# Head outputs of a unit gathered in one tile and turned by four DMA transposes in a two-layer transformer kernel

## The chip, the cores and the metric

The kernel runs on one core of a Trainium2 chip. The metric is the time of one execution on the device, in microseconds. The profile is of one such execution.

## What is computed

Two transformer layers that share their weights, on 2048 tokens of 512 features, all in bf16. Each layer is an attention block (32 heads of 16 features) and a feed-forward block (1376 hidden features), each with a residual. Both blocks normalize their input, the feed-forward block twice.

```python
def _A_ref(x, wqkv, wo):
    B, S, D = x.shape
    H = 32; Dh = D // H
    qkv = (x @ wqkv).reshape(B, S, 3, H, Dh).transpose(2, 0, 3, 1, 4)
    q, k, v = qkv[0], qkv[1], qkv[2]
    scores = jnp.einsum("bhqd,bhkd->bhqk", q, k) * Dh ** -0.5
    p = _softmax(scores, axis=-1)
    o = jnp.einsum("bhqk,bhkd->bhqd", p, v)
    return o.transpose(0, 2, 1, 3).reshape(B, S, D) @ wo

def _B_ref(x, w1, b1, w2, b2):
    h = _gelu(_layernorm(x) @ w1 + b1)
    return h @ w2 + b2

for layer in range(2):
    x = x + _A_ref(_layernorm(x), A_wqkv, A_wo)
    x = x + _B_ref(_layernorm(x), B_w1, B_b1, B_w2, B_b2)
```

## The kernel before

**Who sets the order.** No instruction's place is written by hand. The jobs of the kernel are Python generators that hand tasks to a list scheduler (`Sched`, L271) while the kernel is built. The scheduler keeps a model of each engine with the durations that every task is given, always takes the task that can begin first and, among those ready, the one of lowest priority number (`best`, L380), and so lays out five fixed instruction streams (PE, ACT, DVE, POOL, and SP, the queue of the DMAs). On the chip each stream runs in its order, with semaphore waits where tiles are passed on. A DMA counts in the model as done after its issue time, its latency and a margin of 1.0 us (L25, L126). When the plan is complete, it is run through again, and zero matmuls (`zw`, L1260) are put into the gaps of PE[...].

**Units and segments.** The two attention blocks are called L=1 and L=3. A unit is a set of query tiles of 128 tokens: four units of four tiles in L=1, three of four and two of two in L=3, so 9 in all. A segment is one unit and one head group `hg` of four heads; each unit has eight. In the first unit of each layer the keys come in two parts.

**Scores and exponentials.** For a segment, PE computes scores with keys on the partitions, 128 keys by 512 queries at a time, four heads beside each other in rows of 32 (L1354). ACT takes the exponential of two or three such score tiles per instruction (L1339). Keys of the blocks 3, 6, 9, 12 and 15 can also go to DVE, which forms an approximate exponential out of the bits: one load of the score tile (L1431, `d_load`), then three shifted copies (L1462, `job_d`). Whether it does is decided by `take_d` (L1364) as the plan is laid: it needs DVE to be free within 1.3 us and little work waiting on it, and a free PSUM bank. A tile that DVE doesn't take is left to ACT.

**Values.** PE multiplies the exponentials with the values and a column of ones, 17 output rows per head, in four columns of 32 (L1528). So bank 6 of PSUM holds, for head `hp` of the group, 16 features and the sum of the weights on partitions 32·hp to 32·hp+16, for up to 512 queries. A tile of ACT takes one such product, a tile of DVE four.

**End of a segment** (`job_segend`, L1551). DVE turns the bank in 32x32 blocks into `accT` (L1558): queries on the partitions, features along the row. In the units whose keys come in two parts, POOL keeps the first part's sums in `OT` (L1577) and adds them (L1586 to L1589). Then DVE takes the reciprocal of the weights' sum (L1591), multiplies (L1596) into one of two buffers `ob` whose rows have 16 features and 16 zeros per head, and turns that in 32x32 blocks back into `OT[:, hg, :]` (L1598). The key `oproj` of the unit before holds these steps back until that unit's projection has been planned.

**Output projection** (`job_post`, L1609). When the eight head groups of a unit are turned, PE contracts for each 128 tokens eight planes of `OT` with eight planes of `wo` (L1622). Both have 128 rows, of which 64 are zeros. DVE adds the residual (L1624). The norm, the turn of the normed rows by a DMA (L1647), and the feed-forward block (L1655, L1679, L1685, L1693) follow, beside the next unit's scores. The unit's result then feeds the QKV projection of the second layer (L900), whose keys are stored and loaded turned (`job_kload`, L1136), or the output.

**The last unit** (`job_tail`, L1710). Its feed-forward block can't hide behind scores. It begins when the unit before is done and head groups 0 to 6 are turned; `tail_tile` (L1749) brings the residual into PSUM by an identity matmul (L1754) and adds the eight products of the projection (L1758), of which the last waits for head group 7.

Of the kernel before, what the change touches and what calls it, by code (L numbers as in the profile page):

```python
# [8 lines left out]
BF16 = mybir.dt.bfloat16  # L9
F16 = mybir.dt.float16  # L10
F32 = mybir.dt.float32
# [3 lines left out]
ALU = mybir.AluOpType  # L15
# [244 lines left out]
def I(fn, reads=(), writes=(), dur=0.3, same_ok=(), lat=None):  # L260
    return (fn, tuple(reads), tuple(writes), tuple(same_ok), dur, lat)
# [236 lines left out]
class Builder:  # L498
# [44 lines left out]
    def alloc(self, es):  # L543
# [5 lines left out]
        self.wo = t("wo", [128, 8, 512], BF16)  # L549
# [28 lines left out]
        self.ob = t("ob", [128, 2, 512], BF16)  # L578
# [31 lines left out]
        pl = self.S_.pools  # L610
# [13 lines left out]
        pl["ob"] = Pool([])  # L624
# [105 lines left out]
    def build_startup_late(self):  # L730
# [4 lines left out]
        def fills():  # L735
# [8 lines left out]
            yield f(lambda e: e.memset(self.ob[:, :, :], 0.0), [("ob", 0), ("ob", 1)], 1.3)  # L744
            for k in range(2):
                S_.release("ob", k)
# [4 lines left out]
            yield f(lambda e: e.memset(self.wo[:, 0:4, :].rearrange("p a b -> p (a b)").bitcast(F32), 0.0), [("wo0",)], 1.0)  # L751
            yield f(lambda e: e.memset(self.wo[:, 4:8, :].rearrange("p a b -> p (a b)").bitcast(F32), 0.0), [("wo0",)], 1.0)
# [4 lines left out]
            wor = self.A_wo.rearrange("(g h d) n -> h d g n", h=4, d=16)  # L757
            for hp in range(4):
                yield ld(lambda e, hp=hp: e.dma_start(self.wo[32 * hp:32 * hp + 16, :, :], wor[hp]), [("wo0",)], [("wo", hp)])
            S_.mark(("wld",))  # L760
# [790 lines left out]
    def job_segend(self, sg):  # L1551
# [40 lines left out]
        if self.prev(L, qc):  # L1592
            yield ("keys", [("oproj",) + self.prev(L, qc)])
        o = yield ("get", "ob")
        ob = self.ob[:, o, 0:W].rearrange("p (b r) -> p b r", r=32)
        yield Task("dve", 1.2, [I(lambda e: e.tensor_tensor(out=ob[:, :, 0:16], in0=T[:, :, 0:16], in1=rv.unsqueeze(2).broadcast_to([128, nb, 16]), op=ALU.mult), [RA, ("rv", a)], [("ob", o)], 0.147 + 0.268 * W / 512)])  # L1596
        S_.release("accT", a)
        yield Task("dve", 1.2, [I(lambda e: e.transpose(self.OT[:, hg, 0:W], self.ob[:, o, 0:W]), [("ob", o)], [("OT", hg)], 0.17 + 0.53 * W / 512)])  # L1598
        S_.release("ob", o)
# [3 lines left out]


# [4 lines left out]
    def job_post(self, L, qc):  # L1609
        S_ = self.S_  # L1610
        pr = self.post_prio(L, qc)
        tiles = self.units[L][qc]
        W = 128 * len(tiles)
        if L == 3 and qc == len(self.units[L]) - 1:
            yield from self.job_tail(L, qc)
            return
        yield ("keys", [("ot", L, qc, hg) for hg in range(8)])
        for i, tt in enumerate(tiles):
            yield ("ready", "pe", [("OT", hg) for hg in range(8)])
# [90 lines left out]
    def job_tail(self, L, qc):  # L1710
# [8 lines left out]
        yield ("keys", [("post",) + self.prev(L, qc)] + [("ot", L, qc, hg) for hg in range(7)])  # L1719
        slot = yield ("get", "lnc")  # L1720
# [28 lines left out]
    def tail_tile(self, L, qc, tt, slot, i, left):  # L1749
# [5 lines left out]
        for h0 in range(8):  # L1755
            if h0 == 7:
                yield ("keys", [("ot", L, qc, 7)])
            yield Task("pe", pr if h0 == 7 else 1.5, [I(lambda e, hg=h0: e.matmul(self.ps[:, b, :], lhsT=self.OT[:, hg, i * 128:(i + 1) * 128], rhs=self.wo[:, hg, :], start=False, stop=(hg == 7), skip_group_check=True),  # L1758
                                                        [("OT", h0)] + [("wo", k) for k in range(4)], [("ps", b)], 0.216, [("ps", b)])])
# [112 lines left out]
```

## Time and profile before

| | before |
|---|---|
| Median of 3 runs | 1634.3 us (1631.6 to 1636.0) |
| Span of the profiled execution | 1629.9 us |
| Exponentials on ACT (L1339) | 1302 instructions |
| Score tiles taken by DVE (L1431) | 874 |
| Turns from `ob` to `OT` on DVE (L1598) | 72 |
| Matmuls with `wo` (L1622 and L1758) | 256, of 379 ns from issue to end |
| DMA transposes `xnT`, `yT` (128x512) | 70, 2.5 us from issue to landing |

A line of a group names the source line, the engine, the operation, what it writes and reads with the shapes, and how often it ran; then the busy time in us and the mean duration in ns; then how long the engine sat idle just before these instructions, and what ended most of that. A matmul's duration runs from issue to end, and matmuls overlap, so the 379 ns are not what one more of them adds. Busy time of a queue's DMA transpose is the time in which it holds the SP queue; the landing is given separately.

### The profile page before, as it was taken

Reading aid. Unit: us, or ns where it says so; the run is one execution under the profiler, and the core shown is the slowest. Engines: PE = TensorE matmul, PEld = TensorE weight load, DVE = VectorE, ACT = ScalarE, POOL = GpSimd, SP = SyncE. Lnnn points to the kernel's source line nnn. Section 1 sums busy time; section 2 is a strip of 40 time slices with the busy share of each in tenths; the row PEclk is TensorE's granted clock in tenths of the full one; section 3 lists DMA queues with packets and bytes.
Section 4 is the critical chain, followed back from the end, with each engine's and each line's share of the span. In section 5 each row is a group of like instructions: output and inputs, shape, how many; then the busy total and the mean of one; then the engine's idle time right before and its main releaser. Section 6 shows DMA issues by size and latency. Waiting matters only on the chain.

```text
span 1629.9 us, 39346 instructions
## 1 busy us (share of the span) xinstructions
PE 1591.9 (98%) x16609; PEld 491.6 (30%) x16609; DVE 1484.6 (91%) x3278; ACT 1560.1 (96%) x1385; POOL 379.4 (23%) x575
## 2 busy tenths in 40 slices
PE   9999999999999999999999999999999999999998
PEld 3222222222222222222222222222222222344454
DVE  7899998989999899989989799998898989999893
ACT  6999999999999999989999999999999999999996
POOL 5354231111211022112111125411011101223220
PEclk9999999999999999999999999999999999999999
DMA  6651000202211031223611330010000100010000
GB/s 171 120 124 60 8 11 6 48 20 55 63 21 40 14 68 51 47 47 89 109 29 49 65 85 18 14 21 7 18 8 8 21 9 11 7 17 12 18 11 14
DMA packets 179121, 65.74 MB, mean 40 GB/s; under 512 B 158747, under 2 KB 173312, under 8 KB 178944
## 3 DMA queue, kind: packets, MB, share of 16 engines
q1 hardware_dynamic: 178944, 63.22, 17.3%
q8 instruction: 130, 2.13, 0.6%
q14 instruction: 47, 0.39, 0.1%
HBM read 19.96 MB, written 15.30 MB: 22 GB/s over the span
## 4 chain that ended last, share of the span: by engine, by line
PE 47%; ACT 25%; DVE 25%; issue 2%; POOL 1%; DMA 0%; POOLq 0%; DVEq 0%
ACT PT L1339 22%; PE ps L1354 16%; PE ps L1528 12%; DVE dp L1431 8%; DVE dp L1462 6%; PE ps L1655 4%; PE ps L1693 4%; PE ps L1263 3%; PE ps L900 3%; PE ps L1622 3%; ACT h L1685 2%; DVE accT L1558 1%; PE ps L1267 1%; DVE st L830 1%; PE ps L1265 1%
## 5 line engine op out<-in xcount | busy, mean ns | idle before, releaser
L1339 ACT ACTIVATE PT<-ps 128x1024 bf16<-128x1024 f32 (+1 forms) x1302 | 1481.7, 1262 | 41.1 <-PE ps L1354 35.5
L1354 PE MATMUL ps<-QT,KT 32*128 32x512 bf16 (+1 forms) x4608 | 670.6, 358 | 16.2 <-DVE dp L1431 6.0
L1431 DVE TENSOR_SCALAR dp<-ps 128x512 uint16<-128x512 f32 x874 | 587.4, 680 | 69.4 <-PE ps L1354 66.8
L1462 DVE TENSOR_SCALAR dp<-dp 128x1024 uint16<-128x1024 uint16 (+1 forms) x1341 | 518.0, 429 | 8.0 <-PE ps L1528 3.0
L1528 PE MATMUL ps<-PT,V 128*17 128x512 bf16 (+1 forms) x3619 | 470.2, 358 | 0.4 <-DVE accT L1558 0.4
L1131 POOL TENSOR_SCALAR vs<-V 128x340 bf16<-128x340 bf16 (+3 forms) x240 | 241.5, 1007 | 850.0 <-PE ps L1528 826.9
L1528 PE MATMUL ps<-dp,vs 128*17 128x512 bf16 (+1 forms) x2967 | 428.8, 356 | 3.2 <-DVE dp L1462 2.9
L1354 PEld LDWEIGHTS ps<-QT,KT 32*128 32x128 bf16 x4608 | 168.4, 91 | 541.0 <-ACT PT L1339 263.3
L1528 PE MATMUL ps<-dp,V 128*17 128x512 bf16 (+1 forms) x989 | 207.8, 357 | 2.1 <-DVE accT L1558 1.8
L1265 PE MATMUL ps<-zw 32*128 32x444 bf16 (+1 forms) x709 | 197.6, 325 | 0.1
L1267 PE MATMUL ps<-zw 128*32 128x448 bf16 (+26 forms) x1762 | 158.6, 320 | 1.2 <-DVE dp L1431 1.1
L1528 PEld LDWEIGHTS ps<-dp,vs 128*17 128x17 bf16 x2967 | 109.3, 88 | 126.9 <-issue 97.3
L1528 PEld LDWEIGHTS ps<-PT,V 128*17 128x17 bf16 x3619 | 112.6, 88 | 103.1 <-issue 93.1
L1263 PE MATMUL ps<-zw 128*128 128x448 bf16 (+10 forms) x528 | 126.2, 337 | 3.6 <-DVE ps L709 1.7
L1655 PE MATMUL ps<-yT,wf 128*128 128x512 bf16 (+3 forms) x396 | 101.7, 360 | 1.5 <-DVE h L1679 0.5
L900 PE MATMUL ps<-wqkv,xnT 128*128 128x512 bf16 x336 | 92.3, 382 | 2.0 <-DVE qk L906 1.3
L1679 DVE TENSOR_SCALAR h<-ps,b1c 128x512 bf16<-128x512 f32 (+2 forms) x88 | 61.7, 701 | 6.4 <-PE ps L1655 6.2
L1622 PE MATMUL ps<-wo,OT 128*128 128x512 bf16 x240 | 66.9, 383 | 0.4 <-DVE xres L1624 0.4
L1267 PEld LDWEIGHTS ps<-zw 128*32 128x32 bf16 x1762 | 58.9, 95 | 27.3 <-DVE dp L1431 5.6
L1263 PEld LDWEIGHTS ps<-zw 128*128 128x128 bf16 x528 | 41.6, 98 | 81.6 <-issue 52.9
L1528 PEld LDWEIGHTS ps<-dp,V 128*17 128x17 bf16 x989 | 49.8, 88 | 50.8 <-issue 29.7
L1558 DVE STREAM_TRANSPOSE accT<-ps 128x512 f32<-128x512 f32 (+1 forms) x88 | 57.9, 658 | 3.5 <-PE ps L1528 2.7
(172 smaller groups left out, 927.9 us busy)
## 6 DMA issues: line engine op xcount, KB each, us to landing
wf<-in_B_w_dram SPq DMA_DIRECT2D x90, 128.0 KB, 2.5
q_scr<-qk SPq DMA_DIRECT2D x22, 256.0 KB, 2.1
k_scr<-qk SPq DMA_DIRECT2D x12, 256.0 KB, 2.1
out_dram<-xres SPq DMA_DIRECT2D x16, 128.0 KB, 1.7
xres<-in_A_x_dram SPq DMA_DIRECT2D x7, 256.0 KB, 3.4
v_scr<-vst SPq DMA_DIRECT2D x12, 136.0 KB, 1.8
V<-v_scr SPq DMA_DIRECT2D x8, 204.0 KB, 4.9
wqkv<-in_A_wqkv_dram SPq DMA_DIRECT2D x3, 512.0 KB, 4.4
```

The source lines that it names most:

```text
L900: yield Task("pe", prio, [I(lambda e, c=c: e.matmul(self.ps[:, b, :], lhsT=xnT[:, c, :], rhs=self.wqkv[:, c, which * 512:which * 512 + 512 ...
L1131: yield Task("pool", 0.8, [I(lambda e, k=k: e.tensor_scalar(out=self.vs[:, q, k - 1, i:i + n, :], in0=src, scalar1=WSHIFT[k], scalar2=None ...
L1263: fn = lambda e: e.matmul(self.ps[:, b, 0:w], lhsT=self.zw[:, 0:128], rhs=self.zw[:, 0:w], start=st, stop=st, skip_group_check=True)
L1265: fn = lambda e: e.matmul(self.ps[:, b, 0:w], lhsT=self.zw[32 * p:32 * p + 32, 0:128], rhs=self.zw[32 * p:32 * p + 32, 0:w], start=st, sto ...
L1267: fn = lambda e: e.matmul(self.ps[32 * p:32 * p + 32, b, 0:w], lhsT=self.zw[:, 0:32], rhs=self.zw[:, 0:w], start=st, stop=st, skip_group_c ...
L1339: S_.submit(Task("act", 1e-5 * gi, [I(lambda e, pt=pt, n=n, b0=b0: e.activation(out=self.PT[:, pt:pt + n, :], in_=self.ps[:, b0:b0 + n, :] ...
L1354: return [I(lambda e, kb=kb, i=i: e.matmul(self.ps[:, b, i * W:(i + 1) * W], lhsT=self.KT[32 * hp:32 * hp + 32, hg, kb * 128:(kb + 1) * 12 ...
L1431: self.S_.submit(Task("dve", 0.0, [I(lambda e: e.tensor_scalar(out=self.dp[:, u, w * 512:(w + 1) * 512], in0=self.ps[:, b, :], scalar1=BIT ...
L1462: yield Task("dve", pr, [I(lambda e, k=k, v=v: e.tensor_scalar(out=self.dp[:, v, 0:N], in0=self.dp[:, u, 0:N], scalar1=float(SHIFT[k]), sc ...
L1528: ops.append((nth[j, sh] + 0.1 * i, I(lambda e, hp=hp, v=v, ap=ap[:, i * W:(i + 1) * W], first=first and i == 0, W=W: e.matmul(self.ps[32 ...
L1622: yield Task("pe", pr, [I(lambda e, hg=hg, i=i, b=b: e.matmul(self.ps[:, b, :], lhsT=self.OT[:, hg, i * 128:(i + 1) * 128], rhs=self.wo[:, ...
L1655: yield Task("pe", pr, [I(lambda e, c=c: e.matmul(self.ps[0:M, b, off:off + W], lhsT=self.w1(fc, c), rhs=self.yT[:, c, 0:W], start=(c == 0 ...
```

## The change

DVE no longer turns the head outputs. `ob` becomes one tile for the whole unit, `[128, 16 query blocks, 8 head groups, 16 features]`, and each segment's multiply writes its head group into it. When all eight head groups are there, four DMA transposes, one for each head `hp` of a group, read 32 partitions of `ob` and write `OT[:, hp, :]`: the row of `OT` is now 16·hg + d, so all 128 rows of a plane carry data, and the projection is four matmuls for each 128 tokens. `wo` is loaded in the same order, four planes in eight DMAs, and needs no zeros. The next unit's multiplies wait until these transposes have been planned (key `obt`), no longer for the projection.

In the last unit the transposes take head groups 0 to 6 and the matmuls contract 112 rows. Head group 7 still goes through DVE, from a small buffer `obl` of the old form, and is multiplied with its own padded copy of the weights, which is put into a plane of `OT` that is free by then.

The aim is to take the turns off DVE and half of the projection's matmuls off PE.

```diff
-        self.wo = t("wo", [128, 8, 512], BF16)
+        self.wo = t("wo", [128, 4, 512], BF16)
...
-        self.ob = t("ob", [128, 2, 512], BF16)
+        self.ob = t("ob", [128, 16, 8, 16], BF16)
+        self.obl = t("obl", [128, 256], BF16)
...
-            yield f(lambda e: e.memset(self.wo[:, 0:4, :].rearrange("p a b -> p (a b)").bitcast(F32), 0.0), [("wo0",)], 1.0)
-            yield f(lambda e: e.memset(self.wo[:, 4:8, :].rearrange("p a b -> p (a b)").bitcast(F32), 0.0), [("wo0",)], 1.0)
...
-            wor = self.A_wo.rearrange("(g h d) n -> h d g n", h=4, d=16)
+            wor = self.A_wo.rearrange("(g h d) n -> g d h n", h=4, d=16)
+            for g in range(8):
+                yield ld(lambda e, g=g: e.dma_start(self.wo[16 * g:16 * g + 16, :, :], wor[g]), [], [("wo", g)])
+            S_.mark(("wld",))
+            yield ("keys", [("oproj", 3, 0)])
+            yield f(lambda e: e.memset(self.OT[:, 6, :], 0.0), [("OT", 6)], 0.5)
             for hp in range(4):
-                yield ld(lambda e, hp=hp: e.dma_start(self.wo[32 * hp:32 * hp + 16, :, :], wor[hp]), [("wo0",)], [("wo", hp)])
-            S_.mark(("wld",))
+                yield ld(lambda e, hp=hp: e.dma_start(self.OT[32 * hp:32 * hp + 16, 6, :], wor[7][:, hp, :]), [("OT", 6)], [("wo7", hp)])
...
-        if self.prev(L, qc):
-            yield ("keys", [("oproj",) + self.prev(L, qc)])
-        o = yield ("get", "ob")
-        ob = self.ob[:, o, 0:W].rearrange("p (b r) -> p b r", r=32)
-        yield Task("dve", 1.2, [I(lambda e: e.tensor_tensor(out=ob[:, :, 0:16], in0=T[:, :, 0:16], in1=rv.unsqueeze(2).broadcast_to([128, nb, 16]), op=ALU.mult), [RA, ("rv", a)], [("ob", o)], 0.147 + 0.268 * W / 512)])
-        S_.release("accT", a)
-        yield Task("dve", 1.2, [I(lambda e: e.transpose(self.OT[:, hg, 0:W], self.ob[:, o, 0:W]), [("ob", o)], [("OT", hg)], 0.17 + 0.53 * W / 512)])
-        S_.release("ob", o)
+        if L == 3 and qc == len(self.units[3]) - 1 and hg == 7:
...
+        else:
+            if self.prev(L, qc):
+                yield ("keys", [("obt",) + self.prev(L, qc)])
+            yield Task("dve", 1.2, [I(lambda e: e.tensor_tensor(out=self.ob[:, 0:nb, hg, :], in0=T[:, :, 0:16], in1=rv.unsqueeze(2).broadcast_to([128, nb, 16]), op=ALU.mult), [RA, ("rv", a)], [("ob", hg)], 0.147 + 0.268 * W / 512)])
+            S_.release("accT", a)
...
+    def ot_dma(self, hp, hgs, nb, prio):
+        return self.dma(lambda e: e.dma_start_transpose(self.OT[:, hp, 0:32 * nb].rearrange("p (b r) -> p b r", r=32), self.ob[32 * hp:32 * hp + 32, 0:nb, :, :].rearrange("p b h d -> p (b h d)")),
+                        [("ob", hg) for hg in hgs], [("OT", hp)], prio, 1.31, 1.2)
+    def oproj_mm(self, b, i, hps, K, pr, tail=False):
+        return Task("pe", pr, [I(lambda e, hp=hp: e.matmul(self.ps[:, b, :], lhsT=self.OT[0:K, hp, i * 128:(i + 1) * 128], rhs=self.wo[0:K, hp, :], start=(hp == 0 and not tail), stop=(hp == 3 and not tail), skip_group_check=tail),
+                                 [("OT", hp)] + [("wo", k) for k in range(8)], [("ps", b)], 0.216, [("ps", b)]) for hp in hps])
...
         yield ("keys", [("ot", L, qc, hg) for hg in range(8)])
+        for hp in range(4):
+            yield self.ot_dma(hp, range(8), 4 * len(tiles), pr)
+        S_.mark(("obt", L, qc))
...
-            for h0 in range(0, 8, 2):
-                yield Task("pe", pr, [I(lambda e, hg=hg, i=i, b=b: e.matmul(self.ps[:, b, :], lhsT=self.OT[:, hg, i * 128:(i + 1) * 128], rhs=self.wo[:, hg, :], start=(hg == 0), stop=(hg == 7)),
-                                        [("OT", hg)] + [("wo", k) for k in range(4)], [("ps", b)], 0.216, [("ps", b)]) for hg in (h0, h0 + 1)])
+            for h0 in (0, 2):
+                yield self.oproj_mm(b, i, (h0, h0 + 1), 128, pr)
...
         yield ("keys", [("post",) + self.prev(L, qc)] + [("ot", L, qc, hg) for hg in range(7)])
+        for hp in range(4):
+            yield self.ot_dma(hp, range(7), 4 * n, pr)
...
+        yield ("ready", "pe", [("OT", hp) for hp in range(4)])
+        for h0 in (0, 2):
+            yield self.oproj_mm(b, i, (h0, h0 + 1), 112, 1.5, True)
+        yield ("keys", [("ot", L, qc, 7)])
+        yield Task("pe", pr, [I(lambda e: e.matmul(self.ps[:, b, :], lhsT=self.OT[:, 7, i * 128:(i + 1) * 128], rhs=self.OT[:, 6, :], start=False, stop=True, skip_group_check=True),
+                                [("OT", 7), ("OT", 6)] + [("wo7", k) for k in range(4)], [("ps", b)], 0.216, [("ps", b)])])
```

More of the change, by code (lines that the diff above doesn't have):

```diff
@@ L623, in alloc @@
         pl["accT"] = Pool(range(2))
-        pl["ob"] = Pool([])
         pl["st"] = Pool(range(8))
@@ L743, in fills @@
             S_.release("vst", 0)
-            yield f(lambda e: e.memset(self.ob[:, :, :], 0.0), [("ob", 0), ("ob", 1)], 1.3)
-            for k in range(2):
-                S_.release("ob", k)
+            yield f(lambda e: e.memset(self.obl[:, :], 0.0), [("obl",)], 0.4)
             yield f(lambda e: e.memset(self.bst[:, :], 0.0), [("bst",)], 0.3)
@@ L1591, in job_segend @@
         yield Task("dve", 1.2, [I(lambda e: e.reciprocal(out=rv, in_=T[:, :, 16]), [RA], [("rv", a)], 0.245)])
-        if self.prev(L, qc):
-            yield ("keys", [("oproj",) + self.prev(L, qc)])
-        o = yield ("get", "ob")
-        ob = self.ob[:, o, 0:W].rearrange("p (b r) -> p b r", r=32)
-        yield Task("dve", 1.2, [I(lambda e: e.tensor_tensor(out=ob[:, :, 0:16], in0=T[:, :, 0:16], in1=rv.unsqueeze(2).broadcast_to([128, nb, 16]), op=ALU.mult), [RA, ("rv", a)], [("ob", o)], 0.147 + 0.268 * W / 512)])
-        S_.release("accT", a)
-        yield Task("dve", 1.2, [I(lambda e: e.transpose(self.OT[:, hg, 0:W], self.ob[:, o, 0:W]), [("ob", o)], [("OT", hg)], 0.17 + 0.53 * W / 512)])
-        S_.release("ob", o)
+        if L == 3 and qc == len(self.units[3]) - 1 and hg == 7:
+            ob = self.obl[:, :].rearrange("p (b r) -> p b r", r=32)
+            yield Task("dve", 1.2, [I(lambda e: e.tensor_tensor(out=ob[:, :, 0:16], in0=T[:, :, 0:16], in1=rv.unsqueeze(2).broadcast_to([128, nb, 16]), op=ALU.mult), [RA, ("rv", a)], [("obl",)], 0.147 + 0.268 * W / 512)])
+            S_.release("accT", a)
+            yield Task("dve", 1.2, [I(lambda e: e.transpose(self.OT[:, 7, 0:W], self.obl[:, 0:W]), [("obl",)], [("OT", 7)], 0.17 + 0.53 * W / 512)])
+        else:
+            if self.prev(L, qc):
+                yield ("keys", [("obt",) + self.prev(L, qc)])
+            yield Task("dve", 1.2, [I(lambda e: e.tensor_tensor(out=self.ob[:, 0:nb, hg, :], in0=T[:, :, 0:16], in1=rv.unsqueeze(2).broadcast_to([128, nb, 16]), op=ALU.mult), [RA, ("rv", a)], [("ob", hg)], 0.147 + 0.268 * W / 512)])
+            S_.release("accT", a)
         S_.mark(("ot", L, qc, hg))
@@ L1617, in job_post @@
         yield ("keys", [("ot", L, qc, hg) for hg in range(8)])
+        for hp in range(4):
+            yield self.ot_dma(hp, range(8), 4 * len(tiles), pr)
+        S_.mark(("obt", L, qc))
         for i, tt in enumerate(tiles):
-            yield ("ready", "pe", [("OT", hg) for hg in range(8)])
+            yield ("ready", "pe", [("OT", hp) for hp in range(4)])
             b = yield ("get", "mb")
-            for h0 in range(0, 8, 2):
-                yield Task("pe", pr, [I(lambda e, hg=hg, i=i, b=b: e.matmul(self.ps[:, b, :], lhsT=self.OT[:, hg, i * 128:(i + 1) * 128], rhs=self.wo[:, hg, :], start=(hg == 0), stop=(hg == 7)),
-                                        [("OT", hg)] + [("wo", k) for k in range(4)], [("ps", b)], 0.216, [("ps", b)]) for hg in (h0, h0 + 1)])
+            for h0 in (0, 2):
+                yield self.oproj_mm(b, i, (h0, h0 + 1), 128, pr)
             S_.submit(Task("dve", pr - 1, [I(lambda e, tt=tt, b=b: e.tensor_tensor(out=self.xres[:, tt, :], in0=self.ps[:, b, :], in1=self.xres[:, tt, :], op=ALU.add), [("ps", b), ("x", tt)], [("x", tt)], 0.68)]),
@@ L1754, in tail_tile @@
         yield Task("pe", 1.5, [I(lambda e: e.matmul(self.ps[:, b, :], lhsT=self.ident[:, :], rhs=self.xres[:, tt, :], start=True, stop=False, skip_group_check=True), [("ident",), ("x", tt)], [("ps", b)], 0.216)])
[L1755 to L1759, printed above, removed]
+        yield ("ready", "pe", [("OT", hp) for hp in range(4)])
+        for h0 in (0, 2):
[3 more added lines that the diff above has]
+                                [("OT", 7), ("OT", 6)] + [("wo7", k) for k in range(4)], [("ps", b)], 0.216, [("ps", b)])])
         c = 4 * slot + i
```

## The prediction

> **What bounds the kernel now.** I read the page first (busy time by engine, costliest groups), then the groups with their shapes kept apart, the waits, the table by stretches, and last the timeline of the end. The page:
>
> ```profile
> PE 1591.9 (98%) x16609; PEld 491.6 (30%) x16609; DVE 1484.6 (91%) x3278; ACT 1560.1 (96%) x1385; POOL 379.4 (23%) x575
> ```
>
> PE's 98% is no bound: 480 us of it are the zero matmuls of L1263, L1265 and L1267 (126.2 + 197.6 + 158.6), which the plan puts into gaps. ACT is different: nothing on it is filler. The groups by shape (busy us, mean ns, idle before):
>
> ```profile
> L1339 ACT ACTIVATE PT<-ps 128x1536 bf16<-128x1536 f32 x619 | 920.0, 1486 | 23.5 <-PE ps L1354 18.3
> L1339 ACT ACTIVATE PT<-ps 128x1024 bf16<-128x1024 f32 x682 | 717.7, 1060 | 17.6 <-PE ps L1354 17.1
> L1431 DVE TENSOR_SCALAR dp<-ps 128x512 uint16<-128x512 f32 x874 | 587.4, 680 | 69.4 <-PE ps L1354 66.8
> ...
> L1462 DVE TENSOR_SCALAR dp<-dp 128x1024 uint16<-128x1024 uint16 x1281 | 504.3, 435 | 7.9 <-PE ps L1528 3.0
> ...
> L1598 DVE STREAM_TRANSPOSE OT<-ob 128x512 bf16<-128x512 bf16 x56 | 39.1, 698 | 0.0
> ...
> L1596 DVE TENSOR_TENSOR ob<-accT,rv 128x256 bf16<-128x256 f32 x56 | 24.1, 430 | 0.0
> ...
> L1462 DVE TENSOR_SCALAR dp<-dp 128x512 uint16<-128x512 uint16 x60 | 15.5, 294 | 0.1
> ...
> L1598 DVE STREAM_TRANSPOSE OT<-ob 128x256 bf16<-128x256 bf16 x16 | 6.9, 433 | 0.1
> ```
>
> The reader is to see that the exponentials leave ACT almost no gap (41 us idle before them in 1630), and that DVE shares the same work: L1431 and L1462 compute score tiles that ACT then does not. The two engines are one pool: a microsecond freed on DVE can become an exponential fewer on ACT. Two rows of the stretches (PE, PEld, DVE, ACT, POOL busy) show how full ACT is in the middle:
>
> ```profile
> 430.00:610.00 180.00, 177.70 (x1654) 47.78 (x1656) 163.08 (x358) 178.50 (x155) 32.91 (x43) 1.00 0.15 36
> ...
> 1160.00:1340.00 180.00, 178.33 (x1768) 47.97 (x1766) 167.11 (x365) 179.19 (x155) 24.36 (x23) 1.00 0.06 12
> ```
>
> So ACT bounds 99% of such a stretch. The exceptions are 610 to 1160 us, where ACT waits for PE's scores for 9.1 + 5.9 + 3.7 us, and the end:
>
> ```profile
> 1594.92 0.28 DVE L1596 TENSOR_TENSOR ob<-accT,rv 128x128 bf16<-128x128 f32 x1
> ...
> 1608.37 3.62 PE L1758 MATMUL ps<-wo,OT 128*128 128x512 bf16 x16
> 1609.30 0.45 DVE L1598 STREAM_TRANSPOSE OT<-ob 128x256 bf16<-128x256 bf16 x1
> ```
>
> Here PE works off 14 output-projection matmuls (3.04 us in the chain that ended last) although the last head group is turned at 1609.75.
>
> **What the Trainium skill says.** "VectorE: DVE Perf Modes", section "The three transpose paths", has a DVE transpose in 32x32 blocks at 311 ns for 128x128 and the DMA path at 1309 ns. The trace has 698 ns for four times that area on DVE; a DMA transpose of 128x512 keeps its queue 1.27 us and lands after 2.5 us. "DMA: Bandwidth & Descriptors", section "Anatomy of one DMA", puts a fixed cost of about 2 us on a DMA, most of it completion (for the GpSimd path); this trace's transposes on the SP queue agree in kind:
>
> ```profile
> L877 SPq DMA_TRANSPOSE xnT<-xn x40: 1189/1265/2484, 30.7 to 941.5; - x40
> ...
> DMA to landing us min/median/max: 2.4/2.5/4.3
> ```
>
> "TensorE: Matmul & The Clock Gate", section "Back-to-back issue gap", gives N/2.4 + 2.5 ns, so 216 ns for 512 columns, with no term for the contracted rows. The trace agrees: 14 matmuls in 3.04 us are 217 ns each, and half of their rows hold zeros.
>
> **The change, part by part.** The counts are those of the changed kernel as built, set against the kernel before.
>
> DVE loses 56 transposes of 698 ns and 16 of 433 ns, 46.0 us, and gets one of 433 ns for the last head group. The multiply into the gathered tile has the same elements (256 per partition, 32-byte runs, only further apart), so its 430 ns stay.
>
> The plan spends this at once. Exponentials on ACT go from 619 to 614 (1536 wide), from 682 to 678 (1024 wide) and from 1 to 0 (512 wide): 24 score tiles move to DVE. ACT: 5 x 1.486 + 4 x 1.060 + 0.63 (the 512-wide one, by the difference of the other two) = 12.3 us less. DVE: 24 x 0.680 + 54 x 0.435 - 36 x 0.294 = 29.2 us more, so in sum 46.0 - 0.4 - 29.2 = 16.4 us less. DVE doesn't become the bound by this.
>
> PE loses 128 matmuls with wo and gains 2: 126 x 0.217 = 27 us. Each moved tile needs four value products in place of one: 69 more of 512 columns and 6 of 256; four run side by side, so (69 x 0.217 + 6 x 0.108) / 4 = 4 us. PE gets 23 us looser, most of which the zero matmuls fill again. Price on the path: nothing in the full stretches, since ACT ends them; in 610 to 1160 it helps a little. I credit 1 us, about half of the 1.8 us that ACT idles around the projection at 640 to 650 us.
>
> The 36 DMA transposes are new: 9 units x 4, each 32 partitions x 2048 elements (64 KB in the two half units, else 128 KB). The trace has no transpose with 32 source partitions. From below: the 128x512 ones of the same 128 KB, 1.27 us of queue and 2.5 us to landing. From above: those of 256 KB (KT), 3.2 us to landing, and the slowest of 128 KB, 4.3 us. I take 2.5. Behind the waiting transposes in the SP queue stand the loads of queries (L1103), of weights and the stores; the query loads are issued about two segments (some 20 us each) ahead and DVE waited for none, so 36 x 1.27 = 46 us of queue in 1630 hurts nothing.
>
> Each projection now starts later: from the last multiply 3 x 1.27 + 2.5 = 6.3 us where 0.7 us were. What waits for it is the unit's norm and feed-forward, which run beside the next unit's scores. Two places have a deadline. Unit 2 of the first layer feeds the keys of the second (first key load 771 us; the first layer's last head group is turned only at 826 us, some 10 us behind its last scores), and unit 3 feeds its last key tiles (last KT transpose 956 us; needed from about 980 us). Both have over 20 us of room for the 6 us. Hence 0.
>
> The real danger is the order: PE takes its instructions in a fixed order, so a projection matmul whose DMA is late stops the scores behind it, and ACT after them. The plan counts 1.31 + 1.2 + 1.0 us from issue to use (the duration and latency in the new helper, and the margin on every DMA). 2.5 us fit with 1 us to spare, 3.2 still fit.
>
> At the end, the transposes wait for head group 6's multiply. Before it stood at 1594.9 us; in the changed order only four L1462, one xres and the last group's steps come after it on DVE, after the next-to-last xres (1601.6 us before). I put it at 1603.2 us; the fourth transpose lands at 1609.5 us, six matmuls are then left, the last two for group 7, ending about 1611.2 us against 1612.0 us. With 3.4 us to landing nothing is gained. I credit 0.5 us.
>
> The start (two zero fills of wo on POOL fewer, eight loads of 64 KB in place of four of 128 KB, both for a projection at 245 us) costs nothing: ACT's exponentials hide it.
>
> Sum: -12.3 - 1 - 0.5 = -13.8 us; 1634.3 - 13.8 = 1620.5 us.
>
> **The rivals.** First, PE bounds more than I grant: the 18.7 us of ACT's waits between 610 and 1160 us are cut by half, as the projection is: another 8.4 us, 1612 us. For it: 23 us less real work on PE. Against: feed-forward and QKV matmuls, not the projection, fill most of those stretches.
>
> Second, the moved tiles don't pay: each goes through a single spare bank, DVE already sat 66.8 us waiting for such scores, and if a moved tile costs ACT 0.5 us of waiting, 24 of them eat the 12.3 us: about 1633 us. Against: ACT's waits are named PE, never DVE, and DVE's load falls.
>
> Third, slower: with 32 source partitions the transpose is slow. At twice KT's 3.2 us the use comes 2.9 us after the plan's 3.5; less one exponential that ACT still has in hand (1.3 us) that is 1.6 us in each of 8 units, 13 us, and about 3 us at the end: 1634.3 - 13.3 + 16 = 1637 us. At 8 us to landing it is (8 - 3.5 - 1.3) x 8 = 26 us and 4.5 us at the end: 1651.5 us. The middle is 1644 us. For it: an unseen shape. Against: the transposes of the other four shapes land by their size alone, from 2.5 to 4.3 us at the median.
>
> **How the numbers follow.** Main case 0.62 (1620.5 us), PE relief 0.16 (1612 us), no gain 0.10 (1633 us), late transposes 0.12 (1644 us). Faster is the first two, 0.78; same 0.10; slower 0.12. A plan laid anew shifts small waits by some 5 us either way, so the range goes from 1607 us to 1636 us: below lies a strong form of the relief, above it most of the slower case.
>
> **What would show it.** ACT busy near 1548 us and DVE near 1468 us; idle before L1339 still about 41 us or less, named PE and not DMA; the new transposes at about 1.27 us of queue and 2.5 us to landing; no row of PE waiting for DMA OT of more than a few us; about 3 us between the last exponential's products and the first norm at the end. If PE waits tens of us on those DMAs, or ACT's idle grows by what its busy time lost, I am wrong.

## The result, and the profile after

| | before | after |
|---|---|---|
| Median time | 1632.9 us (1631.6 to 1636.0) | 1620.8 us (1619.6 to 1623.1) |
| Ratio to before, 95% interval | | 0.9925 (0.9905 to 0.9944) |
| Span of the profiled execution | 1629.9 us | 1618.5 us |
| Exponentials on ACT: number, busy | 1302, 1481.7 us | 1292, 1470.1 us |
| ACT idle before them | 41.1 us | 43.2 us |
| ACT's wait for the first products of the last feed-forward (`h<-ps,b1c`) | 12.5 us | 10.9 us |
| Score tiles taken by DVE (L1431) | 874 | 898 |

The change takes 12.1 us off the median, 0.75%. One more execution of the kernel before, taken beside it, is why the time before is now 1632.9 and not 1634.3 us.

The three rows of ACT account for the profiled gain: -11.6 us of exponentials, +2.1 us of idle time before them, -1.6 us at the end, in sum -11.1 of the 11.4 us between the spans. What is left of the span (94.6 us before, 94.3 us after) is the start, the rest of the end and the other work of ACT. I use this sum below for every kernel; what is left lies between 90 and 97 us in all of them. The exponentials of both kernels, all shapes in one line, before and after:

```profile
L1339 ACT ACTIVATE PT<-ps 128x1024 bf16<-128x1024 f32 (+1 forms) x1302 | 1481.7, 1262 | 41.1 <-PE ps L1354 35.5
...
L1339 ACT ACTIVATE PT<-ps 128x1024 bf16<-128x1024 f32 (+1 forms) x1292 | 1470.1, 1262 | 43.2 <-PE ps L1354 36.5
```

The page of the changed kernel, busy time by engine:

```profile
PE 1559.8 (96%) x16214; PEld 482.4 (30%) x16349; DVE 1471.6 (91%) x3249; ACT 1548.6 (96%) x1375; POOL 380.3 (23%) x574
```

ACT lost 11.5 us and DVE 13.0 us. The zero matmuls stayed as they were (195.2 + 145.9 + 141.4 = 482.5 us, 482.4 before). PE shows 32.1 us less, but that is not all relief: 135 of its matmuls have no record in this trace (16214 matmuls for 16349 weight loads; before, 16609 of each), which at 0.217 us each can be up to 29 us. A kernel below with the same other work and more zero matmuls has a complete trace, with PE busy for 1583.8 us. So PE lost 8 us at least, and how much more is not known.

The groups of the changed kernel by shape (busy us, mean ns, idle before and its releaser):

```profile
L1339 ACT ACTIVATE PT<-ps 128x1536 bf16<-128x1536 f32 x614 | 911.7, 1485 | 23.3 <-PE ps L1354 16.9
L1339 ACT ACTIVATE PT<-ps 128x1024 bf16<-128x1024 f32 x678 | 713.4, 1060 | 19.9 <-PE ps L1354 19.6
L1431 DVE TENSOR_SCALAR dp<-ps 128x512 uint16<-128x512 f32 x898 | 600.6, 679 | 66.3 <-PE ps L1354 62.3
...
L1462 DVE TENSOR_SCALAR dp<-dp 128x1024 uint16<-128x1024 uint16 x1335 | 522.3, 432 | 12.7 <-PE ps L1528 8.0
...
L1600 DVE TENSOR_TENSOR ob<-accT,rv 128x256 bf16<-128x256 f32 x56 | 25.0, 447 | 0.1
...
L1462 DVE TENSOR_SCALAR dp<-dp 128x512 uint16<-128x512 uint16 x24 | 6.7, 314 | 0.0
```

24 score tiles went from ACT to DVE: five exponentials of three tiles, four of two and one of one are gone. The waits of ACT that carry a name are still for PE, and DVE's wait for scores (66.3 us, 69.4 before) is no longer than it was. The multiply into the gathered tile costs 447 ns in place of 430.

The stretches (length, then busy time and instructions of PE, PEld, DVE, ACT and POOL, the granted clock of PE, and the DMA share):

```profile
430.00:610.00 180.00, 175.16 (x1599) 47.16 (x1616) 165.43 (x359) 178.96 (x156) 32.82 (x46) 1.00 0.18 46
...
980.00:1160.00 180.00, 171.87 (x1645) 46.93 (x1658) 167.13 (x364) 170.27 (x153) 52.75 (x71) 0.98 0.08 18
1160.00:1340.00 180.00, 174.32 (x1705) 49.20 (x1718) 157.22 (x342) 178.15 (x154) 26.72 (x25) 1.00 0.08 16
```

In the full stretches ACT is as full as before (178.96 and 178.15 of 180 us). The stretch from 980 us is not: ACT's wait for scores there grew from 3.7 to 8.3 us, and the clock is 0.98 where it was 1.00. In 790 to 980 us it grew from 5.9 to 8.3 us, and in 610 to 790 us it fell from 9.1 to 5.7 us.

The new transposes of the changed kernel, by tile and by line (the first is the time on the SP queue in ns, min/median/max):

```profile
L1609 SPq DMA_TRANSPOSE OT<-ob x36: 1182/1274/2196, 245.0 to 1592.9; - x36
...
  PEld ps L1614: 0.9, 2
  PE ps L1614: 0.5, 2
...
DMA to landing us min/median/max: 2.3/2.8/5.0
```

The waits of PE that are named after them are two of a weight load and two of a matmul, 1.4 us in the whole execution. And the end of the changed kernel (start us, us):

```profile
1588.73 0.29 DVE L1600 TENSOR_TENSOR ob<-accT,rv 128x128 bf16<-128x128 f32 x1
...
1589.05 5.73 SPq L1609 DMA_TRANSPOSE OT<-ob  x4
...
1597.77 0.40 PE L1528 MATMUL ps<-PT,V 128*17 128x256 bf16 x8
...
1598.10 1.47 PE L1614 MATMUL ps<-wo,OT 112*128 112x512 bf16 x6
...
1599.27 0.45 DVE L1596 STREAM_TRANSPOSE OT<-obl 128x256 bf16<-128x256 bf16 x1
...
1599.77 0.60 PE L1775 MATMUL ps<-OT 128*128 128x512 bf16 x2
...
1600.20 1.30 DVE L1779 BATCH_NORM_STATS2 st<-ps 128x6 f32<-128x512 f32 x2 [0.48 <-PE ps L1775]
```

The four transposes are issued from 1589.1 to 1594.8 us. PE comes to its first two projection matmuls at 1597.0 us and to the other six at 1598.1 us, and waits for no DMA before them; the two of head group 7 end at 1600.4 us. That is 3.0 us after the end of the last exponential (1597.36 us). Before, the last projection matmul ended at 1612.0 us, 4.8 us after the last exponential (1607.18 us). The first norm begins 2.0 us after the last exponential's value products (1598.17 us), and before it was 3.4 us. The first gelu of the end starts 8.67 us after the last exponential, 10.24 us before: the same 1.6 us or so.

### The profile page after: what moved, and what is told of

The parts are those of the page before. It is cut to its first block, busy times and chain, and to the rows that moved or that the text cites. A ratio compares the mean times of both kernels' runs of the same rounds, so it can differ in the third digit from the quotient of the medians.

```text
span 1618.5 us, 38733 instructions
## 1 busy us (share of the span) xinstructions
PE 1559.8 (96%) x16214; PEld 482.4 (30%) x16349; DVE 1471.6 (91%) x3249; ACT 1548.6 (96%) x1375; POOL 380.3 (23%) x574
## 4 chain that ended last, share of the span: by engine, by line
PE 46%; DVE 25%; ACT 25%; issue 2%; POOL 1%; DMA 1%; SPq 0%; POOLq 0%; DVEq 0%
ACT PT L1339 23%; PE ps L1354 16%; PE ps L1528 13%; DVE dp L1431 9%; DVE dp L1462 6%; PE ps L1707 4%; PE ps L1669 4%; PE ps L1263 3%; PE ps L900 3%; DVE accT L1558 1%; ACT h L1699 1%; PE ps L1267 1%; PE ps L1265 1%; DVE QT L1116 1%; DVE n L965 1%
## 5 line engine op out<-in xcount | busy, mean ns | idle before, releaser
L1339 ACT ACTIVATE PT<-ps 128x1024 bf16<-128x1024 f32 (+1 forms) x1292 | 1470.1, 1262 | 43.2 <-PE ps L1354 36.5
L1431 DVE TENSOR_SCALAR dp<-ps 128x512 uint16<-128x512 f32 x898 | 600.6, 679 | 66.3 <-PE ps L1354 62.3
L1462 DVE TENSOR_SCALAR dp<-dp 128x1024 uint16<-128x1024 uint16 x1359 | 528.1, 430 | 12.8 <-PE ps L1528 8.0
L1528 PE MATMUL ps<-PT,V 128*17 128x512 bf16 (+1 forms) x3594 | 476.9, 358 | 0.3 <-ACT PT L1339 0.2
L1265 PE MATMUL ps<-zw 32*128 32x444 bf16 (+2 forms) x718 | 195.2, 325 | 0.0
L1263 PE MATMUL ps<-zw 128*128 128x448 bf16 (+14 forms) x610 | 145.9, 336 | 2.7 <-DVE ps L709 1.7
L1267 PE MATMUL ps<-zw 128*32 128x448 bf16 (+14 forms) x1462 | 141.4, 326 | 0.3
L1669 PE MATMUL ps<-yT,wf 128*128 128x512 bf16 (+3 forms) x356 | 94.3, 357 | 7.1 <-issue 5.1
L1267 PEld LDWEIGHTS ps<-zw 128*32 128x32 bf16 x1462 | 50.7, 95 | 21.4 <-DVE dp L1431 3.0
L1265 PEld LDWEIGHTS ps<-zw 32*128 32x128 bf16 x718 | 54.1, 92 | 1.2
```

The costliest lines, as they stand in the source:

```text
L1263: fn = lambda e: e.matmul(self.ps[:, b, 0:w], lhsT=self.zw[:, 0:128], rhs=self.zw[:, 0:w], start=st, stop=st, skip_group_check=True)
L1265: fn = lambda e: e.matmul(self.ps[:, b, 0:w], lhsT=self.zw[32 * p:32 * p + 32, 0:128], rhs=self.zw[32 * p:32 * p + 32, 0:w], start=st, sto ...
L1267: fn = lambda e: e.matmul(self.ps[32 * p:32 * p + 32, b, 0:w], lhsT=self.zw[:, 0:32], rhs=self.zw[:, 0:w], start=st, stop=st, skip_group_c ...
L1339: S_.submit(Task("act", 1e-5 * gi, [I(lambda e, pt=pt, n=n, b0=b0: e.activation(out=self.PT[:, pt:pt + n, :], in_=self.ps[:, b0:b0 + n, :] ...
L1431: self.S_.submit(Task("dve", 0.0, [I(lambda e: e.tensor_scalar(out=self.dp[:, u, w * 512:(w + 1) * 512], in0=self.ps[:, b, :], scalar1=BIT ...
L1462: yield Task("dve", pr, [I(lambda e, k=k, v=v: e.tensor_scalar(out=self.dp[:, v, 0:N], in0=self.dp[:, u, 0:N], scalar1=float(SHIFT[k]), sc ...
```

## The experiments

The theory: the time follows the score tiles that DVE takes off ACT, and the plan can take them since the turns are gone. Against it stood these rivals: the relief of PE or the end brings the gain, not the tiles; DVE's relief alone gains nothing; the transposes cost waits; and, added later, spells in which PE has half its clock hide part of the gain, or the plan as such, laid anew by any edit, is the cause. Ratios and times are set against the kernel before, run beside each on the same chip. Where a fragment of a line is shown in a diff, the rest of the line is unchanged.

**The change, with DVE's tiles held at the old number.** `take_d` refuses a tile once DVE has as many in this unit as it had before.

```diff
+CAPS = [0, 82, 113, 108, 112, 77, 28, 117, 122, 57, 58]
...
+        if self.ndseg.get(CAPKEY(sg["i"]), 0) >= CAPS[CAPKEY(sg["i"])]:
+            return None
+        self.ndseg[CAPKEY(sg["i"])] = self.ndseg.get(CAPKEY(sg["i"]), 0) + 1
```

> The whole change, but in each unit DVE may take no more score tiles than it took in the kernel before: 874 in all, 82, 113, 108 and so on by unit, where the change takes 898. DVE and PE keep all their relief, ACT keeps its old 1302 exponentials or one or two off. Theory (the gain is the 24 tiles moved off ACT): only the end is shorter, by 1.5 us; 1631.4 us against 1632.9 before. Rival A (a looser PE or DVE pays by itself, with the same work on ACT): the gain stays, 1621 to 1624 us.

Measured: 1633.1 us, ratio 1.000 (0.9991 to 1.0008). Its groups by shape:

```profile
L1344 ACT ACTIVATE PT<-ps 128x1536 bf16<-128x1536 f32 x619 | 918.7, 1484 | 23.5 <-PE ps L1359 16.9
L1344 ACT ACTIVATE PT<-ps 128x1024 bf16<-128x1024 f32 x682 | 717.2, 1060 | 19.1 <-PE ps L1359 18.6
L1439 DVE TENSOR_SCALAR dp<-ps 128x512 uint16<-128x512 f32 x874 | 585.4, 681 | 94.5 <-PE ps L1359 91.0
```

The counts are the old ones, 619, 682 and 874. DVE has 38.7 us less to do than before (1445.9 against 1484.6) and waits 25 us longer for scores; ACT is about as busy and as idle as before (1483.2 us and 42.6 us), each 1.5 us more, and the shorter wait at the end (11.2 us in place of 12.5) does not make up for that. So in this plan the turns and the halved projection are worth nothing by themselves: the gain goes through the tiles. It is one plan, and plans of one kernel differ by some 5 us (below); the 12 us that are gone are more than twice that.

**DVE's relief without PE's.** Each matmul of the projection is followed by one with zeros, so PE keeps its work. (The last unit is left as changed.)

```diff
-            for h0 in (0, 2):
-                yield self.oproj_mm(b, i, (h0, h0 + 1), 128, pr)
+            for hp in range(4):
+                yield self.oproj_mm(b, i, hp, 2, 128, pr)
...
rhs=self.wo[0:K, hp, :] if r == 0 else self.zz[0:K, :]
```

> The change with each of its projection matmuls followed by one on zeros, outside the last unit, so that PE has its old 8 per 128 tokens; only DVE is relieved. The plan gives DVE 892 tiles, 18 more than before. Theory: 18 x 0.51 us (12.3 us for 24 tiles) and 1.5 us at the end, so about 1622 us. Rival B (the halved projection is what pays): about 1631 us, with ACT's waits for scores between 610 and 1160 us back at 19 us or more.

Measured: 1630.5 us, ratio 0.9988 (0.9979 to 0.9997), 8 us above what the theory said. The group of the exponentials, all shapes in one:

```profile
L1341 ACT ACTIVATE PT<-ps 128x1024 bf16<-128x1024 f32 (+1 forms) x1295 | 1475.4, 1260 | 50.9 <-PE ps L1356 43.5
```

18 tiles moved (892 on DVE) and 6.3 us of exponentials are gone, but ACT idles 9.8 us longer before the others. The stretches show where some of that is, a spell of half clock:

```profile
375.00:380.00 5.00, 4.04 (x35) 0.94 (x34) 5.00 (x9) 4.76 (x5) 2.93 (x3) 1.00 0.43 88
380.00:385.00 5.00, 4.97 (x30) 1.04 (x26) 4.16 (x11) 3.50 (x3) 0.00 (x0) 0.54 0.18 28
385.00:390.00 5.00, 5.00 (x37) 1.01 (x33) 3.32 (x11) 3.51 (x3) 0.08 (x1) 0.50 0.01 3
```

ACT is busy for 7.0 of these ten microseconds, where a full stretch has 9.9. That is 2.9 of the 9.8 us; the rest is spread. This looked like the rival, and the second plan below was made to see whether it was.

**PE's relief alone, two ways.** First the kernel before with half of the projection left out: head groups 4 to 7 aren't multiplied with `wo`, outside the last unit. DVE keeps its turns.

```diff
-            for h0 in range(0, 8, 2):
+            for h0 in (0, 2):
...
stop=(hg == 3)
```

> The kernel before with DVE's turns as they were, but four of the eight projection matmuls left out outside the last unit (the projection's second four head groups are left out of the result). Only PE is relieved. The plan gives DVE 887 tiles, 13 more than before. Theory: 13 x 0.51 us, so about 1626 us. Rival B: about 1621 us, the whole gain. Rival C (PE's relief is worth nothing, only DVE's): about 1633 us.

Measured: 1626.0 us, ratio 0.9962 (0.9948 to 0.9975). DVE took 887 tiles.

Then the changed kernel with 71 idle turns on DVE, each after a multiply, of the old shapes and into a tile that nobody reads:

```diff
+            yield Task("dve", 1.2, [I(lambda e: e.transpose(self.dz[:, 0:W], self.wo[:, 0, 0:W]), [("ob", hg)] + [("wo", k) for k in range(8)], [("dz",)], 0.17 + 0.53 * W / 512)])
```

> The change with a turn of the old size put back on DVE behind each multiply, from wo into an unused tile (71 of them); the DMA transposes and the halved projection stay. The plan gives DVE 893 tiles. Theory: time follows the tiles that ACT keeps, 19 x 0.51 us and 1.5 us at the end: about 1622 us, with DVE busy some 40 us longer than in the change. Rival D (DVE's freed time is worth something by itself on the chip): about 1630 us or more.

Measured: 1628.7 us, ratio 0.9977 (0.9968 to 0.9987), not the 1622 us that I expected, with 893 tiles on DVE. The end is another one. ACT's timeline there, with the lines of the last unit's transposes and of its last projection matmuls (start us, us, and the idle time before):

```profile
1592.53 1.28 ACT L1701 ACT_TABLE_LOAD   x1
...
1600.34 5.07 SPq L1611 DMA_TRANSPOSE OT<-ob  x4
...
1607.85 1.03 PE L1616 MATMUL ps<-wo,OT 112*128 112x512 bf16 x3
...
1614.38 1.35 ACT L1763 ACTIVATE h<-ps,b1c 128x256 bf16<-128x256 f32 x3 [17.69 <-PE ps L1671]
```

The table for the gelu is loaded at 1592.5 us and the first gelu waits 17.7 us for PE; the whole wait of this group is 21.5 us, against 10.9 us in the changed kernel. In this plan the feed-forward of the unit before had fallen behind the last scores. The transposes, which come after it, then lie on the path. They are issued from 1600.3 to 1605.4 us, and the projection matmuls follow about 1.3 us apart, like the transposes, with zero matmuls between, so that the profile names PE and not a DMA. PE is done with the residual at 1602.0 us and with the last projection matmul at 1609.1 us; ten matmuls of 0.217 us are 2.2 us, so I estimate that some 5 us of the wait are the transposes'.

Both kernels of this pair gain with the turns still on DVE, in 13 and 19 tiles, which the prediction gives no cause for. So a second plan of each kernel was wanted.

**What a plan is worth: the kernel before, laid anew.** The scheduler works with a duration for each task. The label of the multiply is lowered by 0.01 us, in the kernel before. No instruction's work changes; the plan is another.

```diff
-0.147 + 0.268 * W / 512
+0.137 + 0.268 * W / 512
```

> The kernel before, with nothing changed but the duration that the plan counts for the multiply ahead of the turn, 0.01 us shorter. The plan comes out otherwise, with 885 tiles on DVE in place of 874. Theory: time follows the tiles and the end; 11 x 0.51 us, so about 1627 us, and half of the gain of the change could come from a luckier plan. Rival G (the gain is the change's own; a plan laid anew is worth nothing): 1632 to 1634 us.

Measured: 1626.8 us, ratio 0.9965 (0.9952 to 0.9977), with 885 tiles on DVE and 1476.9 us of exponentials. An edit that changes no work gains 4.3 us against the median beside it (1631.0 us), 5.7 us by the ratio, with eleven tiles moved. A difference of this size between two single plans tells nothing of an edit, then, and it is as much as the half projection gained above.

**The changed kernel and the two halves, laid anew.** The same label is lowered by 0.01 us in the changed kernel, and by 0.03 us in the one with the zero matmuls and in the one with idle turns.

> A second plan of the change: only the duration counted for the multiply is 0.01 us shorter. DVE has 905 tiles. With the second plan of the kernel before (e8_before_label, 1626.8 us) it makes a second pair. Theory: 7 x 0.51 us less than the change, 1617 us, give or take 4 us. Rival G2 (the change drew a lucky plan, as before drew an unlucky one): 1624 us or more.

> A second plan of e2_double_mm (only DVE relieved, PE has its old number of projection matmuls, four of eight on zeros): the duration counted for the multiply is 0.03 us shorter. DVE has 899 tiles, one more than in the change. Theory (tiles set ACT's work, the rest is waits of the single plan): 1618 to 1625 us. Rival B (without PE's relief no gain, however many tiles): 1629 us or more, ACT's waits for scores over 43 us in all as in e2_double_mm.

> A second plan of e4_turns_put_back (DVE's turns put back as idle work, PE relieved): the duration counted for the multiply is 0.03 us shorter. DVE has 888 tiles. In e4_turns_put_back the feed-forward block of unit 3 of the second layer came after the last score and left ACT 10 us more of waiting at the end; in this plan 11 exponentials follow it. Theory: 14 x 0.51 us and 1.5 us at the end, 1624 us, give or take 4 us for waits that a plan shifts. Rival D (DVE's freed time has a worth of its own): 1630 us or more.

Measured: 1618.2 us, ratio 0.9903 (0.9888 to 0.9917) for the changed kernel, which makes it the fastest of all; 1625.4 us, 0.9949 (0.9937 to 0.9960) with the zero matmuls, hardly above the theory's 1618 to 1625; 1624.1 us, 0.9938 (0.9925 to 0.9951) with the idle turns, as the theory had it. The group of exponentials of the fastest kernel:

```profile
L1339 ACT ACTIVATE PT<-ps 128x1024 bf16<-128x1024 f32 (+1 forms) x1289 | 1466.7, 1258 | 46.3 <-PE ps L1354 40.1
```

With 905 tiles on DVE this is 3.4 us less of exponentials than in the changed kernel as it stands, and 3.1 us more of waits. With DVE's relief alone the second plan gains more than the first, but it is not clearly past the kernel before under its other label: the intervals of 0.9949 and 0.9965 overlap. The plans with the old amount of zero work and each transpose once, side by side (us):

| Relieved | tiles on DVE | exponentials | idle before them | wait at the end | ratio |
|---|---|---|---|---|---|
| nothing (the kernel before; other label) | 874; 885 | 1481.7; 1476.9 | 41.1; 44.6 | 12.5; 11.2 | 1; 0.9965 |
| DVE (zero matmuls; other label) | 892; 899 | 1475.4; 1471.8 | 50.9; 46.5 | 11.0; 11.1 | 0.9988; 0.9949 |
| PE (half projection; idle turns; other label) | 887; 893; 888 | 1474.4; 1473.0; 1476.2 | 40.9; 42.0; 40.7 | 10.7; 21.5; 11.2 | 0.9962; 0.9977; 0.9938 |
| both (the change; other label) | 898; 905 | 1470.1; 1466.7 | 43.2; 46.3 | 10.9; 10.8 | 0.9925; 0.9903 |

By rows the mean ratios are 0.998, 0.997, 0.996 and 0.991. In the mean, then, neither half brings what the two together bring. The single plans scatter by 4 to 6 us, though: the best one with PE relieved (0.9938) is as good as the change within the intervals, and a third plan with both reliefs (0.9948, the last one below) puts the mean of that row at 0.993. The number of tiles is clearer than the time: 874 to 893 in the five plans in which DVE has its turns, 892 to 907 in the six in which it hasn't and is free to take tiles. How the halves combine on the chip is not shown. ACT's waits are 46 to 51 us with DVE's relief alone and 41 to 42 us with PE's alone, but with both they go from 41 to 53 us, the plans below included.

**The transposes twice.** In the changed kernel the four transposes of each unit are issued twice (label 0.127, so this too is another plan).

```diff
-        for hp in range(4):
+        for hp in (0, 1, 2, 3, 0, 1, 2, 3):
```

> The change with each group of four transposes issued twice over, the second time to the same place, so that every projection starts some 5 us later and the SP queue holds 46 us more; the duration that the plan counts for the multiply is 0.02 us shorter, which gives a plan with 902 tiles on DVE whose feed-forward block of unit 3 of the second layer ends 10 exponentials ahead of the last score (11 in the change). Theory (the transposes hide): 4 tiles more than the change's 898, so 1618 to 1624 us, and ACT's waits for scores in sum within 5 us of the change's 36.5. Rival E (later projections cost what they are late): 9 x 5 = 45 us at most, 1630 us or more.

Measured: 1624.5 us, ratio 0.9955 (0.9941 to 0.9970), just above the theory's range. By line:

```profile
L1609 SPq DMA_TRANSPOSE OT<-ob x72: 1186/1273/2577, 241.0 to 1599.8; - x72
...
  DVE ob L1600: 3.0, 2
  PEld ps L1614: 0.9, 2
```

Another 46 us on the SP queue add 1.2 us to ACT's wait for scores (37.7 against 36.5 us). The waits named after the transposes are 0.9 us of PE and 3.0 us of DVE's multiply, which writes `ob` anew. 3.4 us more come at the end (ACT waits 14.3 us there), where the second four are issued as late as 1599.8 us. So in these plans the transposes cost the steady part nothing that can be seen, and the rival that wants them to stop PE is out. At the end they can cost something, here and in the plan with idle turns above.

**The spells of half clock.** In its profiled execution the changed kernel has one at about 1035 us, the kernel before has none. With `FILL_U`, which sets how much zero work the plan puts into gaps, at 0.60 in place of 0.55:

```diff
-FILL_U = 0.55
+FILL_U = 0.60
```

The same was done to the kernel with zero matmuls, and once more to the changed kernel with the label at 0.087.

> The change with that number at 0.60. The profile of the change shows 6 us of half PE clock near 1035 us, in which ACT waited. Theory: the spell goes, and with it some 3 to 4 us: 1616 to 1618 us. Rival F (the spell is hidden, or more zero matmuls hold up scores): 1620 us or more.

> The kernel of e2_double_mm with one number changed: zero matmuls fill PE's gaps up to 0.60 of a window where it was 0.55. The order of all other work stays as it was. e2_double_mm ran 12 us at half PE clock from 380 to 392 us, and ACT waited 43.5 us for scores in all. Theory now: ACT's exponentials set the time only as long as ACT's waits stay as before, and the spell at half clock cost e2_double_mm its gain; without it 1622 to 1625 us. Rival B (PE's old load costs it): stays at 1629 to 1631 us with the clock at 1.0.

> The change with the duration counted for the multiply 0.06 us shorter, a plan with 907 tiles on DVE, and zero matmuls up to 0.60 of a window. Theory: 9 tiles more than the change, 4.6 us less work on ACT, so 1613 to 1618 us, the best of both if the waits don't grow. Rival H (more tiles than the change's cost as much in waits as they save): 1620 us or more.

Measured for the changed kernel with more zero work: 1620.3 us, ratio 0.9925 (0.9911 to 0.9939). In its profiled execution the spell is gone (clock 1.00 from 980 to 1160 us), ACT's wait for scores in that stretch is 5.9 us in place of 8.3, and the span is 1.9 us shorter. But a profile is one execution. The five others of this kernel have a mean clock of PE of 0.997 or 0.998 (1.000 is full clock from start to end), as all four of the changed kernel have, and the ratio is the one of the change. So more zero work did not do away with the spells. The kernel with zero matmuls in the projection and more fill: 1630.2 us, 0.9987 (0.9980 to 0.9995); its spell stays in the profiled execution, from 380 to 395 us.

What the lost clock costs is seen between executions of one kernel. Their median times in us, with the number of executions (the kernel before as it ran beside these two, on the same chip):

| | mean clock 1.000 | mean clock 0.997 or 0.998 |
|---|---|---|
| the kernel before | 1630.4 (12) | 1632.6 (8) |
| zero matmuls in the projection, more fill | 1627.6 (7) | 1631.5 (13) |
| the change, more fill | 1618.5 (1) | 1620.3 (5) |

A mean clock of 0.998 is 3.3 us of clock lost in 1630 us, as much as one spell of 6.5 us at half clock loses, and the execution takes 2 to 4 us longer. So a spell costs time, most of the clock that it loses, and the kernel before, too, has executions with a lower clock. But the spells do not hide the gain of DVE's relief either: at clock 1.000 its first plan is 2 us faster than the kernel before beside it, with more fill 2.8 us, where the theory had some 10 us.

The changed kernel with more fill and a label of 0.087: 1625.6 us, 0.9948 (0.9935 to 0.9960), not the 1613 to 1618 us expected from its 907 tiles. Its exponentials:

```profile
L1339 ACT ACTIVATE PT<-ps 128x1024 bf16<-128x1024 f32 (+1 forms) x1289 | 1468.3, 1261 | 52.6 <-PE ps L1354 46.1
```

It has as few exponentials as the fastest kernel, and 6.3 us more of waits before them. So the number of tiles moved doesn't give the time alone. And the spells don't decide between the kernels: the fastest one has two in its profiled execution (mean clock 0.997).

## Why the prediction was right, and where it wasn't

**The bound, right.** ACT's exponentials set the pace, and DVE and ACT are one pool. With the tiles held at the old number the whole change was worth nothing in the plan that was tried, whatever it takes off DVE and PE.

**-12.3 us for the tiles: measured -11.6 us.** The ten exponentials are the predicted ones (619 to 614, 682 to 678, 1 to 0), but these counts were read from the finished plan; only their price was forecast. The term was taken from the durations, and successive exponentials overlap: in the profile before, the durations add up to 619 x 1.486 + 682 x 1.060 + 0.63 = 1643.4 us, and ACT was busy for 1481.7 us, so each overlaps the next by 161.7 / 1302 = 0.12 us. Ten fewer are 12.3 - 1.2 = 11.1 us; the mean of the wide ones, 1485 in place of 1486 ns, adds 0.6 us. DVE was to be 1468 us busy and is 1471.6 us; 0.9 us of that is the multiply's 17 ns more, 56 times.

**-1 us for PE's relief around the projection: wrong in sign.** The idle time before the exponentials grew by 2.1 us. I looked for a fall from 610 to 1160 us. It came in the first part (-3.4 us), and the two others gave more back (+2.4 and +4.6 us). In the profile with more zero work and without the spell the last part has 2.4 us less, so about half of its rise goes with the spell.

**PE's slack priced at nothing "since ACT ends them": not borne out.** I took the freed time of DVE for the only source of moved tiles ("The plan spends this at once") and gave PE's 23 us no price in the full stretches. By that step DVE's relief alone should have brought the gain of the change, and PE's relief alone nothing. DVE's brought 0.1 and 0.5%, PE's 0.2 to 0.6%, the two together 0.75 and 1.0%, and the kernel before under another label 0.35%. A tile that DVE takes needs its scores from PE in a spare bank and four value products for one, so it is plausible that PE's slack decides whether a moved tile pays. It was not shown: how the gain splits stays open, since plans of one kernel differ by as much as the halves do.

**PE's zero matmuls fill most of the slack again: wrong.** They stayed at 482 us. How much looser PE got, the trace with its missing records does not say (8 to 32 us; 23 were forecast). The prediction set its 217 ns for a matmul beside N/2.4 + 2.5 ns. The same section of the Trainium skill, "Back-to-back issue gap" in "TensorE: Matmul & The Clock Gate", calls this the gap of an isolated matmul and has about 131 ns for 512 columns in a stream of matmuls and weight loads. The stream of 14 measured here took 217 ns each; that decides, and the sum stands.

**-0.5 us for the end: measured -1.6 us.** I let the last matmuls wait for the fourth transpose, which was to land some 6 us after the multiply of head group 6, and had both too close to the end. The multiply comes at 1588.7 us, 8.6 us ahead of the end of the last exponential, and in this plan nothing at the end waits for the transposes. So the fewer matmuls count in full: 3.0 us from the last exponential to the last projection matmul, 4.8 us before. The "about 3 us" between the last exponential's products and the first norm in the prediction's last part came out as 2.0 us; it was 3.4 us before.

**The price of the transposes, right.** 1.27 us on the queue, as taken; 2.8 us to landing where I took 2.5, under the 3.5 us that the plan allows. 1.4 us of waits on PE in all. The third rival rested on an unseen form with 32 source partitions, and that form costs nearly what the known one does. In the first plan with idle turns, where the last unit's transposes come late, they lie on the path at the end, as the prediction had assumed for its own case.

**The rivals.** PE's relief cutting waits by half (1612 us) did not come: the waits grew. "The moved tiles don't pay" (1633 us) failed for the change, but it describes its DVE half in the first plan well: 18 tiles, 6.3 us of exponentials, 9.8 us of waits. I had argued against it that ACT's waits are named PE and never DVE; that was no argument, since a PE that serves more tiles of DVE is named PE too.

**The total.** 13.8 us of gain were predicted; the medians give 12.1 us, the spans 11.4 us. The three terms are off by 0.7, 3.1 and -1.1 us, which is 2.7 us too much in sum. That 1620.8 us lies so near to 1620.5 us is luck: the errors of the terms cancel in part, the median of before is 1.4 us lower in its second taking, and single plans differ by more than that. Under the other labels the change gains 0.6% (0.9903 against 0.9965). The line on a plan laid anew, some 5 us either way, was right in size: an edit without work moved the kernel before by 4.3 us and the changed one by 2.6 us.

## What to carry to other kernels

Where a planner shares one kind of work between two engines, time freed on one of them is worth only what it lets the planner move, so ask for the counts of the moved instructions first; with the counts held fixed, the same edits were worth nothing in the plan that was tried. Ask too who feeds the moved work, and don't set its relief at nothing because another engine ends the stretch: the plans with PE's relief alone gained 0.2 to 0.6% here, though for what reason stayed open. A profile is one execution; whether an effect such as a slow spell is gone is read from all of them. And before a gain of 0.4% is put down to an edit, lay the plan of the old kernel anew by an edit that does nothing, and see how far the time moves.

## What the runs showed of the hardware that I had not expected

PE fell to half its clock for 6 to 12 us after stretches in which it was not idle for long. The changed kernel by stretches:

```profile
1030.00:1035.00 5.00, 3.53 (x36) 1.05 (x36) 4.89 (x11) 3.71 (x4) 2.63 (x5) 0.95 0.01 3
1035.00:1040.00 5.00, 5.00 (x35) 0.93 (x34) 3.32 (x8) 3.19 (x3) 0.00 (x0) 0.50 0.26 47
1040.00:1045.00 5.00, 4.99 (x51) 1.22 (x43) 3.87 (x9) 4.13 (x5) 0.00 (x0) 0.87 0.32 58
```

PE was busy for 3.53 of the first 5 us, all of its idle time there being one gap of 1.47 us, from 1031.38 to 1032.85 us, ended by DVE's L1431. The Trainium skill, "TensorE: Matmul & The Clock Gate", section "What's actually happening", gives the half clock to a PE that was idle for at least one window of about 3.4 us. The spell in this trace came after a gap of less than half of that, and no record is missing there (36 matmuls for 36 weight loads); in the kernel with zero matmuls in the projection the longest gap in the 5 us ahead of the spell was 0.83 us. What sets it off isn't settled here. It is not the instructions alone: the kernel before, unchanged, ran with mean clocks from 0.995 to 1.000, and at 0.995 it took some 7 us longer (1637.2 against 1630.4 us on one chip).

A DMA transpose from 32 partitions of 4 KB each takes the SP queue 1.28 us and lands after 2.8 us (medians of the first 24); that of 128 partitions of 1 KB took 1.27 and 2.5 us. The shape of the source made little difference.
